# Sums of weight quarters: their loads and stores issued by GpSimd, and one pair of bank additions moved to VectorE

## The chip, the core and the metric

The kernel runs on one core of a Trainium2 chip. The core has TensorE (PE in the profile), VectorE (DVE), ScalarE (ACT), GpSimd (POOL) and SyncE (SP), each with an instruction stream of its own that is worked off in order, and 16 DMA engines that move data between HBM and the on-chip memory. Any engine's stream may hold the instruction that starts a DMA. The metric is the device time of one execution in microseconds (us); lower is better.

## The reference

An attention over 8 x 12 heads with normalised queries and keys, followed by an MLP mixer: a product over the 448 tokens, then a product over the 768 channels. All in float32.

```python
def rmsnorm(x, g):
    rms = np.sqrt(np.mean(x * x, axis=-1, keepdims=True) + 1e-06)
    return x / rms * g
q_n, k_n = rmsnorm(q, g_q), rmsnorm(k, g_k)              # (8, 12, 448, 64)
scores = np.matmul(q_n, k_n.transpose(0, 1, 3, 2)) / sqrt(64)
attn = exp(scores - max(scores)); attn = attn / sum(attn)
x = np.matmul(attn, v)                                    # heads side by side: (8, 448, 768)
xt = x.transpose(0, 2, 1)
h = np.maximum(xt @ w_tok1, 0.0) @ w_tok2                 # tokens 448 -> 256 -> 448
u = x + h.transpose(0, 2, 1)
h2 = np.maximum(u @ w_ch1, 0.0) @ w_ch2                   # channels 768 -> 1536 -> 768
out = u + h2
```

The weights arrive in float64; the kernel turns them into float32 on the chip.

## The kernel before, in words

The 8 batch elements are worked off one after the other. While the channel products of element b run on TensorE, the attention of element b + 1 is done between them, two heads (a pair) at a time.

The channel products of elements 1 to 7 use a scheme of seven products of quarters in place of eight (`PRODUCTS`): the moving matrix `u` and the weights are cut into four quarters each, and sums of quarters are multiplied too. The moving sums T1 to T4 are made by `moving_sums` (L819; T3 and T4 by GpSimd, L829 and L830), and the sums between the two channel products by `ch1` (among them two additions by GpSimd at L927). The weights' sums of quarters are made once. A weight block has eight slots in HBM (`ws1`, `ws2`, `ws3`): slots 0 to 3 are its plain quarters, slots 4 to 7 the sums that `make` (L209 to L212) computes on GpSimd, four `tensor_tensor` of 128 x 128 per block. There are 36 blocks ("stages"): 18 of the first channel weight, 18 of the second.

Element 0 uses the plain quarters, block by block as they come out of the conversion from float64 (`first_stage`, L894): the block is loaded raw (L181), converted (L273 to L307), used by TensorE, and its plain quarters are stored to HBM (L197). The last 18 blocks (second channel weight) are accumulated in two banks for each of three output channel groups m, in the order 2, 0, 1; when a bank is full, ScalarE copies it out (L903) and GpSimd adds the copy to `u` (L904). The finished channel blocks are transposed by VectorE (`trans_y`, L1015) and stored (L704).

The sums are made in three ways, each a list of items that is merged into the hand-written order:
- `some` (L221), during element 0: blocks 0 to 7. Plain quarters are loaded back into one of two buffers `few` (L226), summed, and the sums stored (L216).
- `direct` (L231), at the end of element 0: the last six blocks, 30 to 35, straight from the converted block into a `raw` buffer (five of these), and stored (L216).
- `one` (L242), from the end of element 0 through element 1: the 22 blocks 8 to 17, 24 to 29, 18 to 23. Each step loads one block (L245), sums the block loaded two steps before, and stores the sums of the step before that (L216).

The weight units that elements 1 to 7 multiply with are loaded from the eight slots by `load_units` (L853), up to eight ahead, a unit with sums only behind the stores of its group's sums.

The order on TensorE, VectorE, ScalarE and GpSimd is the order in which the program is written (`manual_schedule`). SyncE's order is left to the scheduler: nearly all DMAs are issued there, one after another, and one that must wait holds all that stand behind it.

Of the kernel before, what the change touches and what calls it, by code (L numbers as in the profile page):

```python
# [13 lines left out]
ALU = mybir.AluOpType  # L14
# [30 lines left out]
def whole(ctx, tc, shifted, pre, q, k, v, g_q, g_k, moe_w_tok1, moe_w_tok2, moe_w_ch1, moe_w_ch2, out):  # L45


    nc = tc.nc
# [64 lines left out]
    st = dict(pre.st)  # L113
# [39 lines left out]
    def stage_list():  # L153

        l = [(moe_w_ch1, mp, 2 * mp + i, t) for mp in range(KF // 2) for i in range(2) for t in range(KC)]
        return l + [(moe_w_ch2, 3 if m == 2 else 4, m, t) for m in (2, 0, 1) for t in range(KF)]
# [4 lines left out]
    def raw_tile():  # L161
        return raw_pool.tile([P, WCOLS, 2], U32, name="raw")
# [21 lines left out]
    def slots(j, lo, hi):  # L184

        w, group, m, t = stages[j]
        if group < 3:
            a = ws1[group, lo:hi, :, t, m % 2, :]
        elif group == 3:
            a = ws3[lo:hi, :, t, :]  # L190
        else:
            a = ws2[t // 3, lo:hi, :, t % 3, m, :]
        return a.rearrange("q p n -> p q n")
# [8 lines left out]
    def sum_items():  # L202


        n = len(stages)

        def make(a, q):

            nc.gpsimd.tensor_tensor(out=q[:, 6], in0=a[:, 1], in1=a[:, 0], op=ALU.subtract)  # L209
            nc.gpsimd.tensor_tensor(out=q[:, 4], in0=a[:, 1], in1=a[:, 3], op=ALU.add)  # L210
            nc.gpsimd.tensor_tensor(out=q[:, 5], in0=q[:, 6], in1=a[:, 3], op=ALU.add)
            nc.gpsimd.tensor_tensor(out=q[:, 7], in0=a[:, 2], in1=q[:, 5], op=ALU.subtract)  # L212

        def send(i):
            st["summed"].add(i)
            nc.sync.dma_start(out=slots(i, 4, 8), in_=eight(st.pop(("sum", i)))[:, 4:8])  # L216


        FEW = 8

        def some(i):  # L221
            if 2 <= i:
                send(i - 2)
            if i < FEW:
                t = st["sum", i] = x_pool.tile([P, KC, NS, P], F32, name="few", tag="x")
                nc.sync.dma_start(out=eight(t)[:, 0:4], in_=slots(i, 0, 4))  # L226
            if 1 <= i <= FEW:
                q = eight(st["sum", i - 1])
                make(q, q)

        def direct(i):  # L231

            if i < n:
                st["sum", i] = raw_tile()
                make(st["stage", i], eight(st["sum", i]))
            if i > n - 6:
                send(i - 1)


        order = [*range(FEW, n - 18), *range(n - 12, n - 6), *range(n - 18, n - 12)]  # L240

        def one(i):  # L242
            if i < len(order):
                t = st["sum", order[i]] = raw_tile()
                nc.sync.dma_start(out=eight(t)[:, 0:4], in_=slots(order[i], 0, 4))  # L245
            if 0 <= i - 2 < len(order):
                q = eight(st["sum", order[i - 2]])
                make(q, q)
            if 0 <= i - 3 < len(order):
                send(order[i - 3])  # L250
                load_units(st["at"])

        def eight(t):
            if len(t.shape) == 4:
                return t[:].rearrange("p j c n -> p (j c n)")[:, 0:NQ * P].rearrange("p (q n) -> p q n", q=NQ)
            return t[:].rearrange("p n w -> p (n w)").bitcast(F32).rearrange("p (q n) -> p q n", q=NQ)
        return ([(0.0, lambda i=i: some(i)) for i in range(FEW + 2)],
                [(1.0, lambda i=i: direct(i)) for i in range(n - 6, n + 1)],
                [(1.0, lambda i=i: one(i)) for i in range(len(order) + 3)])

    def wide(i):
# [579 lines left out]
    def load_units(u):  # L841

        while ("stage", len(stages) - 1) in st["used"] and st["loaded"] < min(u + UNITS - 1, len(units)):
            i = st["loaded"]
            group, plain, src = units[i]

            if not plain and not has(group, st["summed"]):
                assert i > u  # L850
                break
            st["unit", i] = unit_pool.tile([P, 3, 2, P], F32, name="unit", tag="unit")
            nc.sync.dma_start(out=st["unit", i][:].rearrange("p t i n -> p (t i n)"), in_=src)  # L853
            st["loaded"] += 1
# [10 lines left out]
    def r_tile(i):  # L865
        return r_pool.tile([P, 2 * HS], F32, name=f"r{i}")
# [12 lines left out]
    def natural(o):  # L879
        s = (HB["B11"], HB["T1"]) if o == 0 else (HB["B21"], HB["B22"])  # L880
        return hb[:, s[0]:s[1] + 1:s[1] - s[0]]

    def first_stage(n):

        w, _, m, t = stages[n]
        wide = w is moe_w_ch2
        last = (KF if wide else KC) - 1
        if t == 0:
            st["m", 0], st["m", 1] = m_tile(), m_tile()
        a, u = st.pop(("stage", n)), st["uT", 0]  # L890
        for o in range(2):
            ps = st["m", o][:, 0:S]
            for half in range(2):
                nc.tensor.matmul(  # L894
                    out=ps, lhsT=a[:, o + 2 * half, :],
                    rhs=natural(half)[:, :, t, :] if wide else u[:, half * KC + t, :],
                    start=(t == 0 and half == 0), stop=(t == last and half == 1))
            if t < last:
                continue
            if wide:  # L900

                to, c = u[:, o * KC + m, :], r_tile(1 + o)[:]
                nc.scalar.copy(out=c, in_=ps)  # L903
                nc.gpsimd.tensor_tensor(out=to, in0=to, in1=c, op=ALU.add)  # L904
            else:
                nc.scalar.activation(
                    out=natural(o)[:, :, m, :], in_=ps.rearrange("p (i n) -> p i n", i=2), func=AF.Relu)
        st["used"].add(("stage", n))
# [131 lines left out]
    def middle_items(b):  # L1040

        items = []
        for t in range(KC):
            items += [(us(NJ, S), lambda cc=cc: tok2(b, cc)) for cc in (t, KC + t)]
            if b:
                items.append((0.0, lambda t=t: moving_sums(b, t)))
        if b == 0:
            return items, [(us(4, S), lambda n=n: first_stage(n)) for n in range(len(stages))]
        items += [(us(6, HS), lambda mp=mp, i=i: ch1(b, mp, i)) for mp in range(KF // 2) for i in range(7)]
        double = [(us(6, HS), lambda i=i, j=j: ch2(b, 0, i, j)) for i in range(7) for j in range(2)]  # L1050
        mixing.update(fn for _, fn in items[3 * KC:] + double)
        return items, double
# [34 lines left out]
    stages = stage_list()  # L1087
# [20 lines left out]
    for p in (4, 5):  # L1108
# [7 lines left out]
        out=g_t[:, 0:1], in0=g_t[:, 0:1], scalar=float(D) ** 0.5, in1=g_t[:, 1:2],  # L1116
# [27 lines left out]
    for b in range(B):  # L1144
# [33 lines left out]
        elif b + AHEAD < B:  # L1178
            t = (b + AHEAD) * NPAIR // 2
# [267 lines left out]
```

## Time and profile before

| | |
|---|---|
| median of three runs | 1307.39 us (1304.22 to 1307.74) |
| the profiled execution | 1308.48 us; its span 1306.6 us |
| PE busy | 1260.9 us (97% of the span) |
| DVE, ACT, POOL busy | 763.7, 375.9, 351.3 us |
| mean granted clock of TensorE | 0.99 |
| DMA | 229.59 MB, mean 176 GB/s |
| DMAs for the sums on SP: loads `few` and `raw`, stores | 8, 22 and 36, 256 KB each |
| DMAs issued by GpSimd | 4, of 64 x 4 bytes |

In the lines of a timeline the first column is the start, the second the duration, both in us; then engine, line of the kernel, operation, output<-input, shapes and count; in square brackets how long the engine had been idle before it, and what ended that. In the lists of waits: the engine and line that waited, what it waited for, the sum in us, how often, and the longest. In the tables by stretch: busy time of each engine with the number of its instructions in brackets, the granted clock of TensorE, the share of the DMA engines' time, and GB/s.

### The profile page before, as it was taken

How to read it: one execution, taken by the hardware profiler on the slowest of the kernel's cores; microseconds unless marked ns; L12 is line 12 of the kernel's file. 1: busy time of each engine (PE TensorE's matmuls, PEld its weight loads, DVE VectorE, ACT ScalarE, POOL GpSimd, SP SyncE). 2: the span in 40 equal slices, each digit the busy share in tenths (PEclk: the TensorE clock that was granted, in tenths of full speed). 3: DMA queues.
4: the chain of work that ended last, by engine and by line, in shares of the span. 5: the costliest groups of instructions: out<-in, count | busy, mean ns of one | idle time of the engine just before them, and what ended most of it. 6: DMA issues, size and time to landing. Idle time of an engine off the chain costs nothing.

```text
span 1306.6 us, 20357 instructions
## 1 busy us (share of the span) xinstructions
PE 1260.9 (97%) x7408; PEld 927.2 (71%) x7408; DVE 763.7 (58%) x1205; ACT 375.9 (29%) x752; POOL 351.3 (27%) x575
## 2 busy tenths in 40 slices
PE   5998999989998999999999999999999999999996
PEld 3444444447787687796778777896788868797996
DVE  6998868827774466645676366754656366433212
ACT  6663423214331134302442043312342033200100
POOL 1302410447452222231332122331232123111220
PEclk9999999989998999999999999999999999999999
DMA  9666485899988776695648767685767865386554
GB/s 210 171 186 179 117 225 151 201 260 253 245 197 207 175 168 167 145 248 115 162 130 197 187 150 174 158 226 110 177 157 160 225 139 139 113 225 144 172 172 90
DMA packets 506131, 229.59 MB, mean 176 GB/s; under 512 B 375460, under 2 KB 467620, under 8 KB 506020
## 3 DMA queue, kind: packets, MB, share of 16 engines
q1 hardware_dynamic: 492898, 226.34, 69.6%
q10 hardware_dynamic: 12994, 1.84, 0.8%
q8 instruction: 61, 1.00, 0.3%
q14 instruction: 50, 0.41, 0.1%
q0 software_dynamic: 128, 0.00, 0.0%
HBM read 188.58 MB, written 39.52 MB: 175 GB/s over the span
## 4 chain that ended last, share of the span: by engine, by line
PE 83%; DVE 6%; DMA 4%; SPq 2%; issue 2%; POOL 2%; ACT 1%; DVEq 0%; ACTq 0%; POOLq 0%
PE m_ps L922 26%; PE m_ps L979 25%; PE s_ps L386 9%; PE o_ps L459 8%; PE m_ps L806 5%; PE m_ps L764 2%; PE t_ps L764 2%; PE m_ps L894 2%; DMA raw<-in_moe_w_ch_dram 1%; PE d_ps L439 1%; DVE raw L274 1%; DVE raw L276 1%; PE m_ps L439 1%; DMA hb<-in_q_dram 1%; DVE es L427 1%
## 5 line engine op out<-in xcount | busy, mean ns | idle before, releaser
L979 PE MATMUL m_ps<-hb,unit 128*128 128x224 f32 x1764 | 342.3, 355 | 4.3 <-DVE uT L988 4.3
L979 PEld LDWEIGHTS m_ps<-hb,unit 128*128 128x128 f32 x1764 | 334.5, 191 | 15.6 <-issue 10.5
L922 PE MATMUL m_ps<-tu,unit 128*128 128x224 f32 x1008 | 201.7, 355 | 0.0
L922 PEld LDWEIGHTS m_ps<-tu,unit 128*128 128x128 f32 x1008 | 189.1, 190 | 14.1 <-issue 9.2
L390 ACT ACTIVATE e<-s_ps 128x448 f32<-128x448 f32 x294 | 138.5, 552 | 207.4 <-PE s_ps L386 199.3
L922 PE MATMUL m_ps<-uT,unit 128*128 128x224 f32 x756 | 151.0, 354 | 0.0
L922 PEld LDWEIGHTS m_ps<-uT,unit 128*128 128x128 f32 x756 | 142.3, 190 | 6.7 <-issue 5.3
L386 PE MATMUL s_ps<-qkT 64*64 64x448 f32 x1260 | 143.7, 545 | 0.8 <-ACT x L747 0.8
L459 PE MATMUL o_ps<-e,v 64*64 64x448 f32 x1148 | 129.4, 538 | 0.3 <-ACT uT L496 0.2
L988 POOL TENSOR_TENSOR uT<-uT,r 128x448 f32<-128x448 f32 (+1 forms) x56 | 56.6, 1022 | 229.0 <-DVE r L988 138.5
L427 DVE TENSOR_TENSOR es<-es,e 128x896 f32<-128x896 f32 x90 | 109.1, 1212 | 13.8 <-ACT e L390 8.5
L927 DVE TENSOR_TENSOR r<-m_ps,r 128x448 f32<-128x448 f32 x63 | 39.2, 622 | 108.0 <-PE m_ps L922 55.8
L988 DVE TENSOR_TENSOR uT<-uT,m_ps 128x448 f32<-128x448 f32 (+1 forms) x70 | 33.7, 498 | 114.2 <-PE m_ps L979 114.2
L386 PEld LDWEIGHTS s_ps<-qkT 64*64 64x64 f32 x1260 | 44.9, 132 | 69.0 <-issue 58.7
L459 PEld LDWEIGHTS o_ps<-e,v 64*64 64x64 f32 x1148 | 44.9, 133 | 62.9 <-issue 58.9
L806 PE MATMUL m_ps<-w_sb,h 128*128 128x448 f32 x192 | 78.1, 560 | 10.3 <-DVE uT L811 10.3
L927 POOL TENSOR_TENSOR hb<-r,r 128x448 f32<-128x448 f32 x21 | 24.1, 1147 | 235.8 <-ACT r L943 227.2
L806 PEld LDWEIGHTS m_ps<-w_sb,h 128*128 128x128 f32 x192 | 36.6, 195 | 48.0 <-issue 27.3
L928 ACT ACTIVATE hb<-hb 128x448 f32<-128x448 f32 x63 | 36.3, 577 | 117.3 <-DVE hb L927 98.6
L1329 DVE TENSOR_REDUCE ms<-sq 128x28 f32<-128x896 f32 (+2 forms) x44 | 47.5, 1079 | 35.6 <-ACT sq L1315 32.8
L348 DVE TENSOR_TENSOR qk_t<-qk_t,rs 128x896 f32<-128x896 f32 (+1 forms) x42 | 54.2, 1327 | 15.5 <-POOL rs L1362 15.3
L811 DVE TENSOR_TENSOR uT<-uT,m_ps 128x448 f32<-128x448 f32 x48 | 29.2, 613 | 54.2 <-PE m_ps L806 54.0
(132 smaller groups left out, 1417.5 us busy)
## 6 DMA issues: line engine op xcount, KB each, us to landing
unit<-ws SPq DMA_DIRECT2D x294, 384.0 KB, 4.2
raw<-in_moe_w_ch_dram SPq DMA_DIRECT2D x72, 256.0 KB, 3.7
v<-in_v_dram SPq DMA_DIRECT2D x96, 112.0 KB, 3.8
xs<-xt SPq DMA_DIRECT2D x56, 168.0 KB, 5.0
out_dram<-turned SPq DMA_DIRECT2D x168, 56.0 KB, 1.9
qk_t<-in_q_dram SPq DMA_DIRECT2D x144, 56.0 KB, 3.2
qk_t<-in_k_dram SPq DMA_DIRECT2D x144, 56.0 KB, 3.5
x<-xs SPq DMA_DIRECT2D x42, 192.0 KB, 3.4
```

The source lines that it names most:

```text
L348: nc.vector.tensor_tensor(out=x, in0=x, in1=r.unsqueeze(2).to_broadcast(list(x.shape)), op=ALU.mult)
L386: nc.tensor.matmul(out=pss[i][rows_of(i, a), 0:S], lhsT=qkT[h, 1, k * D:(k + 1) * D], rhs=qkT[h, 0, :], start=True, stop=True)
L390: nc.scalar.activation(out=e[:, i, :], in_=pss[i][:, 0:S], func=AF.Exp)
L427: nc.vector.tensor_tensor(out=es[:], in0=(es if k > 1 else st["e", t, 0])[:], in1=st["e", t, k][:], op=ALU.add)
L459: nc.tensor.matmul(out=st["o", p][a * D:(a + 1) * D, 0:S], lhsT=vt[rows, k * D:(k + 1) * D], rhs=e[rows, :], **kw)
L764: nc.tensor.matmul(out=st["t1", h][jc][:, 0:HC], lhsT=w1_sb[:, c, jc * P:(jc + 1) * P], rhs=st["x", b, h][:, :, c, :], start=start and c = ...
L806: nc.tensor.matmul(out=ps[:, 0:S], lhsT=st["h1", jc][:, cc * P:(cc + 1) * P], rhs=w2_sb[:, jc].rearrange("p c r -> p (c r)"), start=(jc == ...
L922: nc.tensor.matmul(out=ps[:, j * HS:(j + 1) * HS], lhsT=w[:, t, j, :], rhs=m, start=(t == 0), stop=(t == KC - 1))
L927: add = lambda e, o, x, y: e.tensor_tensor(out=o, in0=x, in1=y, op=ALU.add)
L979: nc.tensor.matmul(out=ps[:, j * HS:(j + 1) * HS], lhsT=st["w"](j, t), rhs=hb[:, HB[what], t, :], start=(t == 0), stop=(t == KF - 1))
L988: add = lambda e, o, x, y: e.tensor_tensor(out=o, in0=x, in1=y, op=ALU.add)
L1329: self.nc.vector.tensor_reduce(out=st["ms", p][:, p % 2, lo:hi], in_=sq[:, lo:hi], axis=AX_X, op=ALU.add)
```

## The change

Three `dma_start` move from SyncE to GpSimd's own stream: the store of the sums (L216) and the two loads of plain quarters (L226, L245). They stand there where the program writes them, between GpSimd's computations. These are 30 loads and 36 stores of 256 KB, each of 128 partitions x 4 pieces x 512 bytes. And for the last block of element 0 (channel group m = 1, the last to be finished) VectorE adds both banks to `u` straight from the bank, in place of ScalarE's copy and GpSimd's addition.

```diff
         def send(i):
             st["summed"].add(i)
-            nc.sync.dma_start(out=slots(i, 4, 8), in_=eight(st.pop(("sum", i)))[:, 4:8])
+            nc.gpsimd.dma_start(out=slots(i, 4, 8), in_=eight(st.pop(("sum", i)))[:, 4:8])
...
             if i < FEW:
                 t = st["sum", i] = x_pool.tile([P, KC, NS, P], F32, name="few", tag="x")
-                nc.sync.dma_start(out=eight(t)[:, 0:4], in_=slots(i, 0, 4))
+                nc.gpsimd.dma_start(out=eight(t)[:, 0:4], in_=slots(i, 0, 4))
...
             if i < len(order):
                 t = st["sum", order[i]] = raw_tile()
-                nc.sync.dma_start(out=eight(t)[:, 0:4], in_=slots(order[i], 0, 4))
+                nc.gpsimd.dma_start(out=eight(t)[:, 0:4], in_=slots(order[i], 0, 4))
...
             if wide:
-
                 to, c = u[:, o * KC + m, :], r_tile(1 + o)[:]
+                if n == len(stages) - 1:
+                    nc.vector.tensor_tensor(out=to, in0=to, in1=ps, op=ALU.add)
+                    continue
                 nc.scalar.copy(out=c, in_=ps)
                 nc.gpsimd.tensor_tensor(out=to, in0=to, in1=c, op=ALU.add)
```

In the changed order, as built, SyncE's stream loses these 66 DMAs, and some others trade places in it: in element 1 four unit loads stand ahead of the next pairs' query and key loads, where single ones stood between them. VectorE's two additions stand between the second and third pair of its last transposes of element 0. GpSimd's stream is the old one with the DMAs in their places and without the last two additions of L904. Lines behind L903 move down by two.

## The prediction

> **What bounds the kernel now.** The page comes first: engines, then the slices.
>
> ```profile
> PE 1260.9 (97%) x7408; PEld 927.2 (71%) x7408; DVE 763.7 (58%) x1205; ACT 375.9 (29%) x752; POOL 351.3 (27%) x575
> ```
>
> TensorE is occupied for 97% of the span, so a change can only win where TensorE waits, plus the clock that it loses after a pause. The list of TensorE's waits in 240 to 420 us, the stretch in which the last sums are made, has three entries:
>
> ```profile
> PE m_ps L806 <- DVE uT L811: 6.2, 1, 6.2
> PE m_ps L979 <- DVE uT L988: 4.3, 1, 4.3
> PE m_ps L894 <- DVE stage L307: 1.2, 1, 1.2
> ```
>
> The timelines of POOL, DVE and PE around 280 us show what stands behind the first:
>
> ```profile
> 261.71 0.46 POOL L212 TENSOR_TENSOR raw<-stage,raw 128x128 f32<-128x128 f32 x1
> 270.68 0.46 POOL L209 TENSOR_TENSOR raw<-stage 128x128 f32<-128x128 f32 x1 [8.51 <-DMA ws<-raw]
> ...
> 277.19 0.46 POOL L209 TENSOR_TENSOR raw<-raw 128x128 f32<-128x128 f32 x1 [4.70 <-DMA raw<-ws]
> ...
> 280.73 2.21 POOL L904 TENSOR_TENSOR uT<-uT,r 128x448 f32<-128x448 f32 x2
> ```
> ```profile
> 257.28 1.16 DVE L1015 STREAM_TRANSPOSE turned<-uT 128x448 f32<-128x448 f32 x2
> 281.89 0.65 DVE L1015 STREAM_TRANSPOSE turned<-uT 128x448 f32<-128x448 f32 x1 [23.45 <-POOL uT L904]
> ```
> ```profile
> 284.18 8.36 PE L806 MATMUL m_ps<-w_sb,h 128*128 128x448 f32 x16 [6.18 <-DVE uT L811]
> ```
>
> The last two additions of L904 are ready when ScalarE's copies end (about 265.9), but stand in POOL's stream behind the direct sums and two of `one`; those wait 8.51 and 4.70 us for DMAs that SP issues late. VectorE's transposes wait for the additions, L811 stands behind the transposes, and TensorE waits for L811. (That the last transpose is said to wait for a DMA at 282.98 is the same chain: the second addition ends at 282.94.) The table by stretch adds the clock:
>
> ```profile
> 280.00:285.00 5.00, 0.82 (x1) 0.50 (x2) 2.63 (x5) 0.00 (x0) 4.84 (x9) 0.66 0.92 198
> 285.00:290.00 5.00, 5.00 (x10) 2.45 (x9) 1.57 (x3) 0.00 (x0) 4.64 (x10) 0.66 0.99 347
> ```
>
> The 16 matmuls after the pause take 8.36 us; 24 of the same line take 9.29 at 444.10, which is 6.19 for 16. So the stall costs 6.18 + 2.17 = 8.4 us, 1.35 times its length; I price other stalls by that factor.
>
> **The two additions (L903, L904).** Removed: two copies of ScalarE (0.53 each) and two of POOL (1.1 each), none on a path of their own. Added: two VectorE additions out of a bank, 0.62 each by the same shape at L811. They need the banks (263.8 and 265.3), and VectorE has nothing to do from 258.4 to 281.9, which hides them; without that cover they would cost TensorE 0.1 each, as the banks come free by 0.62 in place of 0.53. The transposes then follow at 266, and L811 waits for its own matmuls alone. Next late behind that is POOL's third L829, treated below. Gain: 8.4 us.
>
> **The 66 DMAs, SP's side.** SP loses 66 issues of some 0.45 us, and its waits for sums (26.8 us for `few`, 8.2 us for `raw` in its list of waits). What gains from it? Up to 175 us the raw weight loads come earlier, but TensorE waits only 1.2 us for a converted block (255.94): 0 to 1.2, taken as 0, since VectorE, busy 18.5 of 20 us in 230 to 250, paces the conversions. The second entry of 4.3 us (411.6) hangs on a key load that SP issues at 407.32, after issuing without a break from 398.3; only one store of sums (0.43 at 406.30) in that run goes. So 0.5 us, with 0 and the whole stall (4.3 x 1.35 = 5.8) as bounds.
>
> **The 66 DMAs, POOL's side.** This decides. An issue on POOL occupies POOL itself, for a time g that the trace shows only for four tiny ones: the busy times of L1234.
>
> ```profile
> L1234 POOL DMA_DIRECT2D g_t<-in_g_q_dram x2: 524/618/712, 1.3 to 2.0; - x2
> L1234 POOL DMA_DIRECT2D g_t<-in_g_k_dram x2: 526/526/526, 2.5 to 3.0; - x2
> ```
>
> They have 64 pieces each, the moved ones 128 x 4 = 512. Lower bound: 0.53 us, if the cost does not grow with pieces (on SP it does not: 512 pieces of `few` take 0.36 to 0.46, 128 pieces of a unit 0.45). Upper bound: eight times as much, 4.2 us. I take twice the row, 1.05, near the lower end: it is the row of the same engine and instruction, and the pieces need something.
>
> In element 0, `some` has slack: after the Newton steps (149.9) six rounds of store, landing of 3.0, load and sums of 1.8 (4.8 + 2g), then 1.8 + 2g, end at 180.5 + 14g = 195, against L904's first need at 222.4 and the reload of x into those buffers at 226.0. It binds only from g = 3.0.
>
> From 247.6 (end of the second pair of L904) the queue is counted through. The first two direct sums end at 254.1, as now. Up to the third L829 follow 11 sums of 1.78 (19.6), two pairs L829 and L830 and one L829 (3.1), 21 DMAs, and a wait for the first load, 4.0 after its issue with two more issues in between (4.0 - 2g): 254.1 + 19.6 + 3.1 + 4.0 + 19g = 280.8 + 19g. TensorE multiplies with T3 at 308.43 now, 300.0 with the stall gone. So it fits up to g = 1.01. Next, L927's second addition, which VectorE needs before a bank comes free: plus L830 0.6, two rounds 3.6 + 4g, L927 2.2, VectorE 0.6: 287.8 + 23g, needed by 320.98 - 8.4 = 312.6; fits up to 1.08. After that four rounds and four additions per block of seven products, 11.5 + 8g against 22.0 us on TensorE for the first: in step up to 1.3. At g = 1.05 the stall is 0.75 us, 1.0 with the clock.
>
> The unit loads behind the sums have room: block 11's sums go out at about 274.1 + 15g = 290 (four sums 7.1, nine issues, the first landing 4.0 - 2g, five sums 8.9 and eight issues behind 254.1) and land by 294; SP then issues the query loads that it now issues from 311.0 (302.6 with the stall gone). DMA traffic stays the same in bytes.
>
> VectorE slows POOL: the first direct sum takes 0.63, 0.90, 0.90 and 0.53 beside the conversions, 0.46 each elsewhere. The Trainium skill, "SBUF — State Buffer", section "A bandwidth-pool intuition that's wrong (but worth ruling out)", speaks against the change: a DMA that GpSimd issues needs its descriptors written by GpSimd, and beside a VectorE `tensor_copy` took about 3100 ns in place of 620. By that page the two stores beside the last conversions (to 255) would be 2.5 us later each, an estimate of 5 us in the queue, 6.7 with the clock, and the sum 1306. No run here shows such a DMA yet.
>
> **Sum.** 1308.48 (the profiled execution) - 8.4 - 0.5 + 1.0 = 1300.6; the median shown lies 1.1 under that execution, so 1299.5.
>
> **Rivals.** First, on the other side: POOL's stream becomes the bound. Place: the third L829 and L927 of element 1. The stall is the larger of 19g - 19.2 and 23g - 24.8, plus 8g - 10.5 in the next block, times 1.35. It eats the gain at g = 1.33 and decides from 1.45 (over 0.3% slower): 1.5 gives (9.7 + 1.5) x 1.35 = 15, so 1313; 2.0 gives (21.2 + 5.5 + 2.3) x 1.35 = 39, so 1338; 4.2 gives (72 + 23 + 20) x 1.35 = 155, so 1454. For it: the pieces, eight times the row. Against it: SP's flat issue cost, POOL idle 73% of the span. Second: the transfers. DMA is busy 100% of 300 to 350 us; with element 1 starting 8.4 us earlier the same bytes have less time, each landing on POOL (two per round) takes 5 to 6 us rather than 4, and the gain is given back: 1304 to 1311. Against: units are loaded up to eight ahead, and TensorE waits for none now. Third: SP in its new order holds query and value loads behind four unit loads that wait for sums; this costs from 278.1 + 15g > 302.6, g = 1.63, or from landings 10 us late: 1312 to 1320.
>
> **How the numbers follow.** About 0.3% (3.9 us) is what a measurement here can tell from no change. Forecast (g to 1.2): 0.50. Transfers, or g between 1.2 and 1.45: 0.14, the same within 0.3%. POOL the bound: 0.30, SP's order: 0.06, both slower. The likeliest case alone spans 1293 (the 4.3 us stall gone as well: 1307.4 - 8.4 - 5.8) to 1303.5. The range reaches up to 1325 (g = 1.8), which leaves out about one in five: the wider half of POOL's case above, and a little below.
>
> **What would show it.** Right: no wait of L806 for L811 near 276; VectorE's two additions near 265; POOL's DMAs at about 1 us each; the third L829 ending before TensorE's first product with T3; POOL's idle time before L209 for a store gone. Wrong: issues of 1.5 us and more, POOL busy without a gap from 250 to 400, TensorE waiting for POOL at L922, or for units; new lower clock behind these waits.

## The result: within 0.15% of the kernel before, and the profile after

The changed kernel takes 1309.05 us (median of 12 runs, 1304.18 to 1310.65) against 1307.20 for the kernel before in the same session; the ratio is 1.0015, 95% interval 1.0003 to 1.0028. The forecast of 1299.5 was wrong: the kernel did not become faster. The profiled execution took 1309.72 us, its span 1307.9, which is 1.3 more than the span before.

The engines, from the page of the changed kernel:

```profile
PE 1263.4 (97%) x7408; PEld 925.0 (71%) x7408; DVE 770.3 (59%) x1207; ACT 374.7 (29%) x750; POOL 401.9 (31%) x639
```

POOL is busy 50.6 us longer; its 66 DMAs take 50.7. Their groups of the changed kernel (busy sum in us, mean ns of one, then the idle time before them and what ended it; the group left out here, the eight stores of `few`, takes 6.3 us):

```profile
L216 POOL DMA_DIRECT2D ws<-raw x28 | 21.6, 772 | 0.2
L245 POOL DMA_DIRECT2D raw<-ws x22 | 16.7, 758 | 4.1 <-DMA ws<-raw 4.0
...
L226 POOL DMA_DIRECT2D few<-ws x8 | 6.1, 761 | 18.0 <-DMA ws<-few 17.7 <-ACT e L390 0.3
```

So g, the time per DMA, is 0.77 us. TensorE's waits from 200 to 440 us, changed kernel (sum, times, longest):

```profile
PE m_ps L981 <- DVE uT L990: 3.6, 1, 3.6
PE m_ps L981 <- DMA unit<-ws: 3.4, 1, 3.4
PE t_ps L771 <- DMA x<-xs: 2.5, 1, 2.5
PE m_ps L924 <- DVE r L929: 2.0, 1, 2.0
PE m_ps L894 <- DVE stage L307: 1.8, 2, 1.5
PE m_ps L894 <- ACT r L905: 0.4, 1, 0.4
```

The wait of 6.2 us for L811 is gone. Yet the sum of this list is 13.7 us, and that of the same list before is 13.9 (6.2, 4.3, 2.2 and 1.2): the waits were exchanged, not removed. The 2.2 us of the list before lie at 222 us, ahead of the stretch that the prediction's list covers:

```profile
PE m_ps L894 <- ACT r L903: 2.2, 1, 2.2
```

Three are new: for the load of `x`, for VectorE's L929, and for a weight unit.

Where the time went can be read from the start of the same product in both traces (changed minus before, one profiled execution of each):

| product | before | after | lead (-) or lag (+) |
|---|---|---|---|
| L894, 16 products | 213.89 | 213.78 | -0.1 |
| L459 behind the next L894 | 230.29 | 226.70 | -3.6 |
| L764, first with x | 265.07 | 262.41 | -2.7 |
| L806, first | 274.83 | 278.80 | +4.0 |
| L386 behind L806 | 292.48 | 287.91 | -4.6 |
| L924 with uT | 313.08 | 310.80 | -2.3 |
| L981 behind the wait for the key load | 415.92 | 412.99 | -2.9 |
| L764 of element 2 | 434.67 | 435.99 | +1.3 |

Behind 436 us the lag stays at 1.3 us to the end, so the table holds the whole difference. The lines of the changed kernel's TensorE timeline that make its steps:

```profile
269.77 2.64 PE L771 MATMUL t_ps<-x,w_sb 64*128 64x384 f32 x4 [2.48 <-DMA x<-xs]
...
308.42 2.54 PE L924 MATMUL m_ps<-tu,unit 128*128 128x224 f32 x12 [2.02 <-DVE r L929]
...
412.99 6.49 PE L981 MATMUL m_ps<-hb,unit 128*128 128x224 f32 x24 [3.65 <-DVE uT L990]
422.88 13.27 PE L981 MATMUL m_ps<-hb,unit 128*128 128x224 f32 x60 [3.39 <-DMA unit<-ws]
```

- Element 0 gains 3.5 us near 222, where TensorE waited 2.2 us for ScalarE's copy before, with a low clock behind it (0.86 and 0.80 over 220 to 230 us), and waits 0.4 now at full clock; 0.9 is given back at the last conversions (253).
- The new wait for `x` costs 6.6 us (-2.7 to +4.0): 2.48 of waiting, 3.4 by the low clock behind it (worked out below), and 0.7 that these rows don't explain.
- The wait for L811 is gone: 8.5 us (+4.0 to -4.6).
- L929 takes 2.3 back: VectorE's addition there starts 2.1 us earlier than before (307.79, was 309.87), while TensorE is 4.6 us earlier. The wait near 411 is 0.65 shorter.
- The wait for the unit costs 4.2 (-2.9 to +1.3).

The clock behind the wait for `x`, by stretch (the column behind POOL is the granted clock):

```profile
265.00:270.00 5.00, 2.52 (x10) 1.13 (x9) 0.00 (x0) 0.87 (x2) 3.27 (x5) 1.00 1.02 305
270.00:275.00 5.00, 4.86 (x8) 2.04 (x8) 0.00 (x0) 0.00 (x0) 2.54 (x6) 0.56 0.96 217
275.00:280.00 5.00, 5.00 (x13) 2.75 (x12) 0.00 (x0) 0.98 (x2) 4.83 (x11) 0.76 0.94 315
```

The clock is 0.50 in every microsecond from 271 to 277. At half speed, 0.56 and 0.76 over 5 us are 4.4 and 2.4 us, 6.8 in all, which lose 3.4 us of work.

Two of the new waits can be followed back. First, `x`. SyncE's order before, from its timeline:

```profile
262.06 2.42 SPq L723 DMA_DIRECT2D x<-xs  x3
264.53 1.24 SPq L726 DMA_DIRECT2D x<-xs  x2
265.87 3.57 SPq L216 DMA_DIRECT2D ws<-raw  x4
```

The stores of the last blocks' sums stood behind the five loads of `x`. In the changed kernel GpSimd issues them as the sums are done:

```profile
256.90 0.77 POOL L216 DMA_DIRECT2D ws<-raw  x1
...
261.97 0.77 POOL L216 DMA_DIRECT2D ws<-raw  x1
...
264.53 1.51 POOL L216 DMA_DIRECT2D ws<-raw  x2
```

SyncE issues the loads of `x` from 261.07 to 265.16, in the midst of them. The DMAs on `x` between 225 and 275 us land in 5.2 us at the median (6.8 at most; the line is shown with the experiments). Before (minimum, median, maximum):

```profile
DMA to landing us min/median/max: 3.2/3.5/5.2
```

The three of 192 KB near 262 us alone land in 6.5 us at the median, in place of 4.0.

Second, the unit. GpSimd's timeline of the changed kernel at the last store of sums:

```profile
398.15 0.77 POOL L216 DMA_DIRECT2D ws<-raw  x1
412.50 0.27 POOL L1361 TENSOR_TENSOR nt<-rs 128x56 f32<-128x56 f32 x1 [13.58 <-DVE rs L1353]
...
416.69 0.80 POOL L216 DMA_DIRECT2D ws<-raw  x1
```

The sums of the last block are ready at 398.2, but their store is the next item of the list, and in GpSimd's stream the Newton steps of the next pair (twelve short instructions on the factors that normalise its queries and keys) stand ahead of it, and they wait for VectorE until 412.5. The store goes out at 416.69, SyncE's unit loads behind it at 419.69, and TensorE, which needs the unit at 419.5, gets it at 422.88. SyncE's timeline of the changed kernel has

```profile
419.69 2.24 SPq L853 DMA_DIRECT2D unit<-ws  x5
```

Before, SyncE issued that store (with the one before it) at 411.5, and the unit loads at 418.00:

```profile
411.54 1.55 SPq L216 DMA_DIRECT2D ws<-raw  x2
```

### The profile page after: what moved, and what is told of

Same layout as the page of the kernel before. It is cut to its first block, busy times and chain, and to the rows that moved or that the text cites. A ratio compares the mean times of both kernels' runs of the same rounds, so it can differ in the third digit from the quotient of the medians.

```text
span 1307.9 us, 20329 instructions
## 1 busy us (share of the span) xinstructions
PE 1263.4 (97%) x7408; PEld 925.0 (71%) x7408; DVE 770.3 (59%) x1207; ACT 374.7 (29%) x750; POOL 401.9 (31%) x639
## 4 chain that ended last, share of the span: by engine, by line
PE 86%; DVE 5%; DMA 3%; SPq 1%; issue 1%; POOL 1%; ACT 1%; ACTq 0%; DVEq 0%; POOLq 0%
PE m_ps L924 25%; PE m_ps L981 25%; PE s_ps L386 9%; PE o_ps L459 9%; PE m_ps L894 6%; PE m_ps L806 5%; PE t_ps L764 2%; PE m_ps L764 2%; PE d_ps L439 1%; PE m_ps L439 1%; DVE es L427 1%; DMA raw<-in_moe_w_tok_dram 1%; DVE ms L1331 1%; DVE raw L274 1%; DVE raw L276 1%
## 5 line engine op out<-in xcount | busy, mean ns | idle before, releaser
L981 PE MATMUL m_ps<-hb,unit 128*128 128x224 f32 x1764 | 343.1, 356 | 7.1 <-DVE uT L990 3.6
L981 PEld LDWEIGHTS m_ps<-hb,unit 128*128 128x128 f32 x1764 | 334.9, 191 | 18.8 <-issue 14.2
L924 PE MATMUL m_ps<-tu,unit 128*128 128x224 f32 x1008 | 202.0, 355 | 2.0 <-DVE r L929 2.0
L924 PEld LDWEIGHTS m_ps<-tu,unit 128*128 128x128 f32 x1008 | 189.0, 190 | 16.5 <-issue 9.2
L924 PE MATMUL m_ps<-uT,unit 128*128 128x224 f32 x756 | 151.0, 354 | 0.0
L924 PEld LDWEIGHTS m_ps<-uT,unit 128*128 128x128 f32 x756 | 142.3, 190 | 6.7 <-issue 3.9
L386 PE MATMUL s_ps<-qkT 64*64 64x448 f32 x1260 | 143.7, 545 | 0.8 <-ACT x L747 0.8
L459 PE MATMUL o_ps<-e,v 64*64 64x448 f32 x1148 | 129.4, 538 | 0.3 <-ACT uT L496 0.3
L929 DVE TENSOR_TENSOR r<-m_ps,r 128x448 f32<-128x448 f32 x63 | 39.2, 622 | 107.8 <-PE m_ps L924 55.7
L386 PEld LDWEIGHTS s_ps<-qkT 64*64 64x64 f32 x1260 | 44.9, 132 | 68.9 <-issue 59.5
L929 POOL TENSOR_TENSOR hb<-r,r 128x448 f32<-128x448 f32 x21 | 23.9, 1136 | 220.8 <-ACT r L945 220.8
L459 PEld LDWEIGHTS o_ps<-e,v 64*64 64x64 f32 x1148 | 44.9, 133 | 62.8 <-issue 58.9
L806 PE MATMUL m_ps<-w_sb,h 128*128 128x448 f32 x192 | 76.4, 552 | 3.3 <-DVE uT L811 3.3
L811 DVE TENSOR_TENSOR uT<-uT,m_ps 128x448 f32<-128x448 f32 x48 | 29.3, 613 | 67.0 <-PE m_ps L806 67.0
L806 PEld LDWEIGHTS m_ps<-w_sb,h 128*128 128x128 f32 x192 | 35.9, 191 | 39.9 <-issue 27.0
```

The lines of the kernel that those rows point to most:

```text
L386: nc.tensor.matmul(out=pss[i][rows_of(i, a), 0:S], lhsT=qkT[h, 1, k * D:(k + 1) * D], rhs=qkT[h, 0, :], start=True, stop=True)
L459: nc.tensor.matmul(out=st["o", p][a * D:(a + 1) * D, 0:S], lhsT=vt[rows, k * D:(k + 1) * D], rhs=e[rows, :], **kw)
L806: nc.tensor.matmul(out=ps[:, 0:S], lhsT=st["h1", jc][:, cc * P:(cc + 1) * P], rhs=w2_sb[:, jc].rearrange("p c r -> p (c r)"), start=(jc == ...
L924: nc.tensor.matmul(out=ps[:, j * HS:(j + 1) * HS], lhsT=w[:, t, j, :], rhs=m, start=(t == 0), stop=(t == KC - 1))
L929: add = lambda e, o, x, y: e.tensor_tensor(out=o, in0=x, in1=y, op=ALU.add)
L981: nc.tensor.matmul(out=ps[:, j * HS:(j + 1) * HS], lhsT=st["w"](j, t), rhs=hb[:, HB[what], t, :], start=(t == 0), stop=(t == KF - 1))
```

## The experiments

Each kernel was timed beside the kernel before; ratios are to that one, with 95% intervals. The kernel before moved between 1305.98 and 1308.25 us from session to session, so rows are to be compared by their ratios. The last column is the sum of TensorE's waits from 200 to 440 us.

| kernel | median us | ratio to before | waits us |
|---|---|---|---|
| changed kernel | 1309.05 | 1.0015 (1.0003 to 1.0028) | 13.7 |
| additions alone | 1305.91 | 0.9997 (0.9986 to 1.0009) | 14.8 |
| DMAs alone | 1308.94 | 1.0017 (1.0007 to 1.0026) | 16.7 |
| early last store | 1304.48 | 0.9986 (0.9972 to 0.9999) | 10.2 |
| x loads on ScalarE | 1309.42 | 1.0020 (1.0009 to 1.0030) | 15.0 |
| both of these | 1305.07 | 0.9972 (0.9961 to 0.9984) | 15.9 |
| and two steps later | 1302.31 | 0.9957 (0.9944 to 0.9970) | 12.6 |
| and keys first | 1300.70 | 0.9949 (0.9933 to 0.9965) | 9.5 |
| early store, `few` on SyncE | 1310.45 | 1.0019 (1.0009 to 1.0029) | 13.2 |
| early store, direct stores on SyncE | 1304.90 | 0.9993 (0.9985 to 1.0002) | 13.0 |
| keys first, without additions | 1303.14 | 0.9979 (0.9968 to 0.9990) | 11.6 |
| keys first, and a third step later | 1295.47 | 0.9897 (0.9879 to 0.9914) | 7.0 |
| keys first, direct stores on SyncE | 1296.47 | 0.9909 (0.9893 to 0.9924) | 8.1 |

### One part alone: the additions

```diff
-            nc.gpsimd.dma_start(out=slots(i, 4, 8), in_=eight(st.pop(("sum", i)))[:, 4:8])
+            nc.sync.dma_start(out=slots(i, 4, 8), in_=eight(st.pop(("sum", i)))[:, 4:8])
```

and the two loads (L226, L245) likewise.

> Only VectorE's two additions; all 66 DMAs stay on SyncE. First theory (the additions end the 6.2 us wait, and what the DMAs bring on GpSimd takes the gain away again): TensorE's wait of L806 for L811 is gone, the first product with a unit starts about 8.4 us earlier than in the kernel before (near 286.5 in place of 294.9), no wait for the load of x near 270, and of the lead at least 5 us are left at the end: 1298 to 1302. Rival (a lead won before 300 us is given back at the key load and at the units of the last group, whoever issues the DMAs): the wait near 411 grows by the lead, and the time is 1305 to 1308.

The wait of L806 is gone, and the first product with a unit starts at 287.07, 7.8 us earlier than before. But the time is 1305.91, the ratio not to be told from 1. Not the key load took the lead back, as the rival had it, but GpSimd. TensorE's timeline:

```profile
302.67 0.65 PE L924 MATMUL m_ps<-tu,unit 128*128 128x224 f32 x2 [1.44 <-POOL tu L829]
...
305.67 7.09 PE L924 MATMUL m_ps<-tu,unit 128*128 128x224 f32 x20 [2.35 <-POOL tu L829]
```

and GpSimd's ahead of the second L829:

```profile
300.17 0.46 POOL L209 TENSOR_TENSOR raw<-raw 128x128 f32<-128x128 f32 x1 [10.46 <-DMA raw<-ws]
```

GpSimd stands 10.46 us before a sum whose load SyncE issues late (at 296.5, behind eight stores of L704 that keep it from 286.45 on), with the next T3 behind it; by 317 us the lead is 0.5. A wait of 1.97 us for a unit, until 422.98, is there too, although SyncE issues the last store at about 412.5: its unit loads stand behind L714, which waits until 417.78 for VectorE. So both theories were half right: the additions end the first wait, and alone they are worth nothing, since the DMAs on SyncE make the next one.

### The other part alone: the DMAs

```diff
-                if n == len(stages) - 1:
-                    nc.vector.tensor_tensor(out=to, in0=to, in1=ps, op=ALU.add)
-                    continue
```

> Only the 66 DMAs on GpSimd; ScalarE's two copies and GpSimd's two additions stay. First theory (the DMAs gain some 3.5 us in element 0 and lose it again at the load of x, and the two additions of L904 still stand behind the sums): TensorE waits about 2.5 us for x near 270 and then still 2 to 4 us for the additions near 280, and the unit wait of about 3 us near 420 is there: 1309 to 1316. Rival (GpSimd's issues are what ends the 6.2 us wait, as they end its waits for stores): no wait of L806 for L811, 1300 to 1306.

The wait of L806 for L811 is 0.46 us, not 2 to 4: with its loads and stores in its own stream GpSimd no longer waits for SyncE and makes L904's additions at 274.53 in place of 280.73. That is the rival's point. The time is 1308.94, just under the first theory's range: TensorE waits 2.4 us for `x`, 1.8 for T3 and 3.9 for the unit. Either part alone nearly ends the wait that the forecast was built on. The wait for `x` comes with the DMAs; a wait for T3 comes with either part alone. And the DMAs alone take the same time as both parts together (1.0017 and 1.0015), so in the changed kernel the additions bring nothing that can be measured.

### The last store ahead of the Newton steps

```diff
-            if 0 <= i - 3 < len(order):
-                send(order[i - 3])
+            if 0 <= i - 3 < len(order) - (i == len(order) + 2):
+                [send(order[k]) for k in (i - 3, i - 2)[:1 + (i == len(order) + 1)]]
```

> The changed kernel with the last store of sums (block 23) issued right behind the sums, ahead of GpSimd's Newton steps of the next pair, 18 us earlier in its stream. First theory (that store holds the units of the last group): the store goes out near 399 in place of 416.7, TensorE's 3.4 us wait for a unit near 420 is gone, and with the clock after it 4.2 us come off: 1304.8. Rival (SyncE is late with the units anyway, by its waits for the stores of xs): the wait stays at 2 us or more, and the time within 1 us of 1309.

1304.48, as expected. The last two stores go out together at 395.21, and of the wait for the unit 0.39 us is left. From a ratio of 1.0015 to 0.9986, each known to 0.0013, this one store is worth 0.29%, 3.8 us; the lead table gave 4.2.

### The load of x

```diff
-            nc.sync.dma_start(out=x[a * D:(a + 1) * D, :, NM, :], in_=xs[NM * P:S])
+            (nc.scalar if (b, half) == (1, 1) else nc.sync).dma_start(out=x[a * D:(a + 1) * D, :, NM, :], in_=xs[NM * P:S])
```

> The changed kernel with the last two of the five loads of element 1's second x (L726) issued by ScalarE, which is idle there, in place of SyncE, where they stand behind three other loads. First theory (the 2.5 us wait for x at 270 costs 6.6 us with the low clock behind it, and the lead is kept): the wait is below 0.7 us, the first product with a unit starts near 284 in place of 290.3, and the time is 1302 to 1305. Rival (VectorE is the bound from 290 to 308 us, and the lead is given back there): TensorE's wait for L929 near 308 grows from 2.0 to 6 us or more, and the time is within 1.5 us of 1309.

The wait for `x` falls to 1.65 us (not below 0.7, as the first theory had it), and with it goes the low clock. All of it comes back at the next engine:

```profile
303.42 5.74 PE L924 MATMUL m_ps<-tu,unit 128*128 128x224 f32 x20 [4.35 <-POOL tu L829]
```

The time is 1309.42. The rival's number, at another place: GpSimd's T3, not VectorE.

> The changed kernel with the last store of sums ahead of the Newton steps and the last two loads of element 1's second x on ScalarE. First theory (leads won before 300 us are given back at GpSimd's third sum T3 and at VectorE's stream near 305, so the x load alone changes where TensorE waits, not how long): the wait for x is below 1.7 us without a lower clock behind it, the wait for T3 near 303 is 3 to 5 us, and the time is 1302.5 to 1304.5, within 2 us of the kernel with the early last store alone. Rival (each wait that goes is worth its length): 6 us less than that kernel, 1298.

With the early last store: 1305.07, and 5.4 us of waits for T3. As the first theory said, a little above its two ranges: with GpSimd this late, the shorter wait for `x` alone brings nothing that shows. A wait for a unit is back, too: 1.99 us, until 406.41.

### GpSimd's queue ahead of T3, and the key loads

Two of the steps that load, sum and store are moved behind T3 and T4 (`sums[5:9]` and `sums[9:20]` become `sums[5:7]` and `sums[7:20]`):

```diff
-                run(merge(begin, sums[5:9]))
-                early, double = merge(early, sums[9:20]), merge(double, sums[20:])
+                run(merge(begin, sums[5:7]))
+                early, double = merge(early, sums[7:20]), merge(double, sums[20:])
```

> As the kernel with both edits before, and two of GpSimd's load-sum-store steps are moved from ahead of the first sums T3 and T4 of element 1 to behind them. First theory (GpSimd's stream is what the lead runs into near 303): the wait for T3 goes, VectorE's L929 is the next with 1 to 3 us, and the time is 1300 to 1302.5. Rival (VectorE is late by as much): a wait of 4 us or more for VectorE near 305, 1302.5 to 1304.5.

The wait for T3 is gone; 4.1 us for VectorE's L929 in two waits, the longer 3.1, stand in its place, more than the 1 to 3 expected. The time is 1302.31.

```diff
-            later(12.0, lambda: load_x(b, half))
+            later(12.0 + 16.0 * ((b, half) == (2, 0)), lambda: load_x(b, half))
```

> As the kernel before it, and the five loads of element 2's first x, which SyncE issues and waits for near 390 us ahead of the next pairs' query and key loads, stand behind them. First theory (the 4.3 us wait near 411 hangs on the key load, and that on SyncE's order): the key load's issue comes 3 to 4 us earlier, the wait falls from 4.3 to about 1 us, and with the clock 3.5 to 5 us come off the kernel before: 1296 to 1299. Rival (the key load waits for a buffer, or VectorE for something else): the wait stays at 3.5 us or more, the time within 1 us of the kernel before.

1300.70, 1.6 us less than the kernel before it, which the two intervals don't tell apart, and short of the 3.5 to 5 expected. The wait for the key pair is 1.73 us, but it had already been 1.94 there, behind a wait of 2.9 for a unit, which is gone; the two together fell by 3.1.

### Whose lead makes the wait for x?

I had put the wait for `x` down to TensorE's lead from element 0, which the chain of `x` doesn't share. If so, `few` back on SyncE must end it.

```diff
-            nc.gpsimd.dma_start(out=slots(i, 4, 8), in_=eight(st.pop(("sum", i)))[:, 4:8])
+            (nc.sync if i < FEW else nc.gpsimd).dma_start(out=slots(i, 4, 8), in_=eight(st.pop(("sum", i)))[:, 4:8])
...
-                nc.gpsimd.dma_start(out=eight(t)[:, 0:4], in_=slots(i, 0, 4))
+                nc.sync.dma_start(out=eight(t)[:, 0:4], in_=slots(i, 0, 4))
```

> The changed kernel with the early last store, and the loads and stores of blocks 0 to 7 back on SyncE: element 0 is then as in the kernel before. First theory (what the DMAs on GpSimd bring in element 0 is eaten by the wait for x near 270 with its low clock): the wait of 2.2 us at the copies near 222 is back, the wait for x is gone, and the time is within 1.5 us of the kernel with the early last store alone: 1303 to 1306. Rival (the lead of element 0 counts): 2.5 us or more slower than that, 1307 or more.

That theory fell. The element-0 wait is back (1.9 us), the wait for `x` is not gone (2.15 and 0.20), and the time is 1310.45. TensorE's lead at its first product with `x` is half of the changed kernel's (1.3 us in place of 2.7, against the kernel before), yet the wait is as long. So element 0's lead is real gain, and most of the lateness of `x` has another reason. The next kernel tries the stores beside it:

```diff
-            nc.gpsimd.dma_start(out=slots(i, 4, 8), in_=eight(st.pop(("sum", i)))[:, 4:8])
+            (nc.sync if i >= n - 6 else nc.gpsimd).dma_start(out=slots(i, 4, 8), in_=eight(st.pop(("sum", i)))[:, 4:8])
```

> The changed kernel with the early last store, and only the six stores of the last blocks' sums (30 to 35) back on SyncE, where they stand behind the five loads of element 1's second x. First theory (TensorE's wait for x near 267 comes from these stores, which GpSimd issues beside the stores of xs and the loads of x): x's loads land in 3.5 us in place of 5, and the wait for x falls from 2.3 to below 1 us with no lower clock behind it; GpSimd waits some 7 us for a buffer instead and is late with T3 near 303 (3 to 5 us): 1303 to 1306. Rival (TensorE is only earlier than x's chain): the wait for x stays at 2 us or more, and T3 is late as well: 1307 or more.

TensorE waits for `x` nowhere, although its first product with `x` starts only 0.5 us later than in the changed kernel (262.94 and 262.41), and the DMAs on `x` from 225 to 275 us land in 3.4 us (the three of 192 KB near 262 in 4.0, in place of 6.5). The tile's landing times, this kernel and then the changed one (minimum, median, maximum):

```profile
DMA to landing us min/median/max: 2.8/3.4/4.2
```
```profile
DMA to landing us min/median/max: 3.6/5.2/6.8
```

So the cause is shown: the six stores of 256 KB that GpSimd issues beside the loads. The edit has two effects more, and their shares aren't separated: SyncE starts the five loads 1.0 us earlier (260.02), and GpSimd's next three loads, which stand behind a store in its stream, move from 266.03 to 269.86. The time is as expected, 1304.90, no better than with the early last store alone: GpSimd waits 8.06 us for a buffer, and TensorE then waits 7.4 for T3, where 3 to 5 were expected. The Trainium skill ("DMA: Bandwidth & Descriptors", section "Issuing engines are not separate DMA queues") says that DMAs run on the same 16 DMA engines and interleave whichever engine started them. The landing times, 3.4 us with the stores held back and 5.2 with them beside, agree.

### What the additions are worth

```diff
-                if n == len(stages) - 1:
+                if False:
```

> As the fastest kernel so far (early last store, two loads of x on ScalarE, two load-sum-store steps later, key loads ahead of element 2's x), but with ScalarE's copies and GpSimd's additions for the last block, as in the kernel before. First theory (with the DMAs in GpSimd's stream the two additions are done early enough, and what VectorE's additions save is some 0.5 to 2 us of GpSimd's time ahead of T3): a wait of L806 for L811 of 0 to 1.5 us, and 1300 to 1303. Rival (VectorE's additions are what the change lives by): a wait of 4 us or more near 276, and 1305 or more.

The first theory fell: L806 waits 4.0 us for L811, and the time is 1303.14, ratio 0.9979 against 0.9949 with the additions. GpSimd makes its additions at 274.40, as early as in the kernel with the DMAs alone, but TensorE, held for `x` for 1.8 us in place of 2.4 and with no low clock behind it, reaches L806 3.7 us earlier (270.72 and 274.37). In the kernel with the DMAs alone the wait for `x` and the low clock behind it had hidden most of this one. So VectorE's additions are worth 0.3% once the rest is mended.

### Two last steps

One more step behind T3 (`sums[5:6]`, `sums[6:20]`), and, apart from it, the direct stores back on SyncE:

> As the fastest kernel (early last store, two loads of x on ScalarE, two load-sum-store steps later, key loads first), with one more load-sum-store step moved behind the first sums T3 and T4. First theory (VectorE, slowed by GpSimd's work beside it, is the bound near 304, not GpSimd's queue): the 3.15 us wait for VectorE stays within 1 us, and the time is within 1.5 us of that kernel: 1299 to 1302. Rival (GpSimd's queue still sets it): the wait falls below 1 us and 3 us or more come off.

> As the fastest kernel, with the six stores of the last blocks' sums back on SyncE behind the loads of x. First theory (waits in a row: one that goes is met again at the next engine): the 1.76 us wait for x is gone, GpSimd is about 5 us later, TensorE waits 2 to 5 us for T3 or VectorE near 304, and the time is within 2 us of that kernel: 1299 to 1303. Rival (the lead at 270 is kept): 1297 to 1298.5.

Both did better than the first theory: 1295.47 and 1296.47. For the first, the rival was right (a wait for VectorE below 1 us, over 3 us off); the second went 0.5 us past its rival. The longest waits of the first:

```profile
PE m_ps L981 <- DVE uT L990: 2.4, 2, 1.8
PE m_ps L894 <- DVE stage L307: 1.7, 2, 1.5
PE m_ps L924 <- DVE r L929: 1.0, 1, 1.0
PE t_ps L764 <- DMA x<-xs: 0.8, 1, 0.8
```

None reaches 2 us, and the granted clock is 1.00 over each 50 us from 250 to 450. VectorE was not the bound by itself: its Newton steps of that pair (L1353 to L1374) take 4.9 us in the kernel before, 5.8 in the changed one, 7.9 in "keys first" and 5.7 here. What GpSimd does beside them may be what stretches them, but no run left them alone there, so that stays argued. In the second kernel the lead won at `x` is kept, with 1.7 us for T3 and 3.1 for L929. The first beats both kernels of this case: 0.9897 of the time before.

## Why the prediction was wrong, step by step

- **The wait of L806 for L811, 8.4 us.** Right: it went, and the lead table shows 8.5. That the two additions bring this gain was wrong: the DMAs alone leave 0.46 us of the wait and take the same time, and the additions alone lose the gain again to T3.
- **g = 1.05.** Measured 0.77, inside the bounds of 0.53 and 4.2. The rival "GpSimd's stream is the bound" needed 1.45. (In that rival's sums, the terms 2.3 and 20 are not derived.)
- **The third L829 at 280.8 + 19g.** With 0.77 that is 295.4; it ended at 302.1. The queue began 2.7 us earlier than counted, but the sum left out three waits of GpSimd for the landing of its own stores (3.0, 0.9 and 3.1 us), had the wait for the first load 0.8 too short, and L829 and L830 took 1.5 each beside VectorE in place of 0.66. It came in time for TensorE's product with it (303.87) only because TensorE's lead was 4.6 us there, not the 8.4 that put the need at 300.0.
- **"What gains from it? ... 0 to 1.2, taken as 0."** Mis-sized: element 0 gained 3.5 us, for another wait than the one asked about. My list of waits began at 240 us and left out the 2.2 us at 222.
- **The failing step: SP's side was asked only for what gains.** The direct stores stood behind the loads of `x` in SyncE's queue; "DMA traffic stays the same in bytes" hid that its order changes. On GpSimd they run beside these loads, and the wait for `x` that follows cost 6.6 us, which the sum had at nothing. This was no rival of mine: the transfers' rival expected longer landings, but for `one` in 300 to 350 us; that the measured time lies in its 1304 to 1311 is luck.
- **"The unit loads behind the sums have room."** Counted for block 11 alone. The end of the list was not counted: the last store waits behind GpSimd's Newton steps, and TensorE's wait for the unit cost 4.2 us. With that store moved the kernel takes 1304.5.
- **The 4.3 us wait, 0.5 us.** Measured 0.65.
- **VectorE at 308 us.** Not in the sum, which had GpSimd's third L829 as the next one late, at 1.0 us with the clock. T3 was in time; VectorE's L929 cost 2.3.
- **The factor of 1.35.** No constant: the wait for `x` cost 2.7 times its length, those for the unit and L929 1.25 and 1.1 times.

With the measured terms (the last is the lead at 213.78): -3.5 + 0.9 + 6.6 - 8.5 + 2.3 - 0.65 + 4.2 - 0.1 = 1.25; the spans differ by 1.3. The forecast's sum was -7.9. The 9.2 between them are the three terms that it left out, 6.6, 4.2 and 2.3, less the 2.6 that element 0 brought net, the 1.0 for T3 that didn't come, and 0.3 in small ones.

## What to carry to other kernels

A DMA that moves to another engine's stream leaves two orders at once: list what it was held behind (here loads that TensorE needed soon), and what it will stand behind (here steps that wait for VectorE), down to the last one of the list. After the stall that a change removes, look for every wait within its length behind it: here three engines were late by nearly as much, and neither the removal alone nor one mended wait paid until the next one was mended too.

## What the runs showed of the hardware

**The low clock comes in whole pieces.** In the stretches read here, TensorE's clock is halved for about 3.4 or 6.8 us after some pauses: 6.8 in the table above, and 3.4 in "keys first" behind 3.15 us of waiting (0.93 and 0.73 over 300 to 310). The length of the pause doesn't decide it. A pause of 1.74 us brought it (the last kernel, for T3):

```profile
295.00:300.00 5.00, 3.26 (x15) 2.62 (x12) 3.90 (x5) 1.58 (x4) 4.98 (x7) 0.83 0.59 187
300.00:305.00 5.00, 5.00 (x24) 4.84 (x23) 3.83 (x5) 2.49 (x5) 4.91 (x7) 0.83 1.16 254
```

and one of 3.80 us did not (additions alone, until 416.21):

```profile
410.00:415.00 5.00, 2.40 (x13) 2.06 (x11) 1.09 (x1) 1.74 (x5) 0.00 (x0) 1.00 1.18 247
415.00:420.00 5.00, 3.79 (x20) 3.80 (x21) 3.05 (x7) 0.49 (x2) 3.40 (x13) 1.00 0.44 89
```

So by these rows a wait of this size costs its length and up to 3.4 us more by the clock. The Trainium skill ("TensorE: Matmul & The Clock Gate", section "Part 1: The HAM clock gate (the "warmup" mystery)") tells of half the clock after an idle window of about 3.4 us, the window running free of the kernel. The pieces of 3.4 and 6.8 us agree, and so does the play of chance; that a whole window must be idle doesn't, since 1.74 us were enough.

**GpSimd's DMA issues beside VectorE.** The 16 DMAs of `few`, issued from 106.8 to 190.6 us, all but two of them while VectorE was at work, took GpSimd 0.75 to 0.89 us each, the rest about the same. The prediction quoted from the Trainium skill ("SBUF — State Buffer", section "A bandwidth-pool intuition that's wrong (but worth ruling out)") that a DMA beside a VectorE `tensor_copy` took 3100 ns in place of 620. No VectorE copy ran beside these, so that case isn't tested; beside the instructions that did run, no issue grew like that. The landing did grow, to 4.3 us for the loads and 3.6 for the stores at the median, from 3.0 and 2.4 when SyncE issued them. But the two loads issued while VectorE stood idle took 4.2 and 4.5, so this doesn't point to VectorE. An issue on GpSimd takes 0.77 us for 512 pieces and 0.52 to 0.71 for the 64 of L1234.
